# The order of weight loads, a scatter and value loads around batch 1 of an attention and feed-forward kernel

## The chip, the cores and the metric

One core of a Trainium2 chip. The time is device microseconds of one execution of the whole program; of several executions the median is taken. Engines are called as in the profile: PE is TensorE, PEld its weight loads, DVE VectorE, ACT ScalarE, POOL GpSimd, SP SyncE. SP computes nothing here; it issues DMAs. POOL issues DMAs too, and does small copies. ACT issues three at the very start.

## The reference

Attention with a window of 32 to both sides and eight global tokens, followed by a feed-forward layer with a squared ReLU:

```python
batch, n_heads, seq, head_dim = (8, 8, 576, 64)      # 8 global tokens
n_tokens, d_model, d_ff = (4608, 512, 2048)

scores = q @ k.T / sqrt(64)                          # each batch and head
mask = (|pos_q - pos_k| <= 32) | is_global[q] | is_global[k]
attn = softmax(where(mask, scores, -1e9))
x = (attn @ v) -> (4608, 512)                        # heads side by side
out = relu(x @ w_in) ** 2 @ w_out
```

All inputs and the output are float32; the kernel computes in float16 with float32 sums.

## The kernel before

The kernel is one list of calls whose order is written out by hand; each engine runs its own part of that list in order. Attention goes by batch (8), by pair of heads (4 a batch, numbered `i` = 0 to 31 over all batches) and by half of the tokens (2 x 288). The feed-forward layer runs over chunks of 512 or 256 tokens, and its pieces (`mm1`: product with `w_in`, ReLU on ACT, square on DVE; `mm2`: product with `w_out`) stand in a list `fills`, from which the attention loops take some after each step, so that PE always has work. A chunk can start when the batch that it needs is done.

A pair of heads goes so: `sc_mm` (L817) makes scores from `kt` and `qt`, `sc_exp` (L826) the exponentials, `sc_mask` (L836) zeroes what the mask forbids, `pv_mm` (L858) sums values and weights, `pv_rec` (L868, L869) makes reciprocals, `pv_mul` (L902) writes the result to `xT`, the input of the feed-forward layer. `xT` holds it transposed, with one column per token; batch 0's first half first goes to a stand-in, `xA`, of which a part is later copied to `xT` (L1055).

Global tokens attend to everything, so their sums come from all pieces of a batch. `pv_sum` and `pv_globals` collect them (`gs`, `gx`, L877 to L894), and `scatter` (L921 to L924) puts them into the columns of `xT` that belong to the global tokens: eight small copies on POOL, each at a column that is read from a register. Batch 0 is scattered twice into `xA`, by two heads at a time, and once, with all, into `xT` (L1061). The feed-forward products of batch 0's second part (`mm1_half(u, 1)`) read `xT` after that.

The data come in three ways:

- Tokens of batches 0 and 1 (`fetch_tokens`) are loaded in rows and transposed by PE (`transpose`, L534, L540), and DVE and ACT put them into `kt` and `qt` (`place_k`, `place_q`, L549 to L568). The tokens of batch 1 are four loads issued by POOL at L1030 to L1033.
- From batch 2 on, POOL copies k and q of a batch within DRAM, cast to float16 (`fetch_batch`, L191, L198: `kscr`, `qscr`), SP adds the global rows (`fetch_batch_globals`, L206), and SP's DMA transposes bring them into `kt` and `qt` (`fetch_transposed`, L214, L215). The global rows are gathered by POOL (`gather_rows`, L465) and stored in DRAM by SP (`gather_store`, L476) as `gscr`.
- Values of batches 0 and 1 go by `fetch_values` (L165) into `stv`, a staging tile in `early`: for a pair of heads two DMAs of 120 KB (L170) and one of 48 KB (L174), 288 KB in all. DVE casts them from there, pair by pair (`cast_values`, L493, called by `values1`). Rows 0 to 7 of `stv` take the values of the global tokens, broadcast from `gscr` by one DMA (L1064). Values of later batches go by POOL (`fetch_batch_values`, L220, into `stf` or `s16b`).

The weights `w_in` and `w_out` are loaded by POOL in four parts each (L307, L310), and cast on the way. A part of `w_out` is 512 KB in float16. `mm2` of chunk 0 uses the four parts in turn, from part 0 on; sums of its quarters (`weight_sum`, L668) are made on DVE after batch 1.

DMAs that POOL issues use eight completion semaphores in turn, as do those of SP and ACT; one that takes a semaphore again waits until the DMA before it on that semaphore has landed.

A tiny DMA, `gate` (L1063), reads the third part of `w_in`. It has no other use than that SP, which issues in order, waits there until this part has landed; behind it stand the broadcast (L1064) and the values of batch 1 (L1068, L1069). POOL's order there is: two scatters into `xA`, four token loads of batch 1 between them, the four parts of `w_out`, the scatter into `xT`, the gathers for batches 2 and 3 (L1070), a memset, and, from the loop over batch 1, the copies of batch 2.

Of the kernel before, what the change touches and what calls it, by code (L numbers as in the profile page):

```python
# [50 lines left out]
def kernel(  # L51
# [10 lines left out]
    nc = tc.nc  # L62
# [9 lines left out]
    NHP = H // 2  # L72
# [92 lines left out]
    def fetch_values(eng, b, hp, to=None):  # L165
        hs = slice(2 * hp, 2 * hp + 2)
        to = stv[:, :, hs] if to is None else to
        n = NT - 1
        for h in range(2):
            eng.dma_start(  # L170
                out=to[8 : 8 + KT, 0:n, h],
                in_=v[b, 2 * hp + h, 0 : KT * n].rearrange("(t s) d -> s t d", s=KT),
            )
        eng.dma_start(  # L174
            out=to[8 : 8 + KN[n], n],
            in_=v[b, hs, KT * n : S].rearrange("h s d -> s h d"),
        )
# [131 lines left out]
    def fetch_w_out(j):  # L309
        nc.gpsimd.dma_start(out=w_out[:, ts(j, 4), :], in_=wo[:, ts(j, 4), :])  # L310
# [292 lines left out]
    def mm1_half(u, half, tiles=range(NDM)):  # L603

        if 0 not in gts:
            gts[0] = sbt("gt", [P, NFF, TC], FP16)
        if 0 in tiles:
            ph_now[u] = pst("mm", [P, 2, 256])
        ph = ph_now[u]
        for j in range(2):  # L610
            for t in tiles:
                halves(
                    ph[:, j], w_in[:, t, (u + j) * P : (u + j + 1) * P],
                    (xT if half else xA)[:, t, half * 256 : half * 256 + 256],
                    start=(t == 0 and j == 0), stop=(t == NDM - 1), skip_group_check=True,
                )
        if NDM - 1 not in tiles:
            return
        rl = sbt("rl", [P, TC], FP16, bufs=5).rearrange("p (j x) -> p j x", j=2)
        nc.scalar.activation(out=rl, in_=ph, func=AF.Relu)  # L620
        nc.vector.tensor_tensor(
            out=gts[0][:, u : u + 2, half * 256 : half * 256 + 256], in0=rl, in1=rl, op=ALU.mult
        )
# [283 lines left out]
    def pv(i, half):  # L907
        pv_mm(i, half)
        pv_rec(i, half)
        pv_sum(i, half)  # L910
        pv_mul(i, half)
        pv_globals(i, half)
# [8 lines left out]
    def scatter(b, pairs=slice(0, NHP), x=xT):  # L921
        xb = x[:, pairs, b * S : (b + 1) * S]
        for g in range(NG):
            nc.gpsimd.tensor_copy(out=xb[:, :, ds(gv[g], 1)], in_=gxs[b][:, pairs, g : g + 1])  # L924
# [125 lines left out]
        mm1_half(u, 0, range(2))  # L1050
    pv(2, 1)
    pv(3, 1)
    for j in range(2):
        fetch_w_out(j)
    nc.scalar.copy(out=xT[:, :, 256:HS], in_=xA[:, :, 256:HS])  # L1055
    for u in range(0, 8, 2):
        fills.pop(0)
        mm1_half(u, 0, range(2, NDM))
    for j in range(2, 4):
        fetch_w_out(j)  # L1060
    scatter(0)  # L1061
    gate = dram.tile([1, 8], FP16, name="gate")
    nc.sync.dma_start(out=gate, in_=w_in[0:1, 0, 2 * 512 : 2 * 512 + 8])  # L1063
    nc.sync.dma_start(  # L1064
        out=stv[0:NG].rearrange("g t h d -> g t (h d)"),
        in_=gscr[("v", 0)][1].rearrange("g h d -> g (h d)").unsqueeze(1).to_broadcast((NG, NT, dm)),
    )
    for hp in range(NHP):  # L1068
        fetch_values(nc.sync, 1, hp)  # L1069
    gs1 = gather_rows(1)  # L1070
    nc.gpsimd.memset(vbs[0][96:P, NT - 1], 0.0)
# [43 lines left out]
    for i in range(2 * NHP, B * NHP):  # L1115
        b, hp = divmod(i, NHP)
# [65 lines left out]
```

## Time and profile before

| | |
|---|---|
| median of 14 executions | 325.36 us (321.3 to 327.66) |
| the profiled execution | 321.33 us, its span 319.6 us |
| PE, DVE, ACT, POOL busy | 309.4, 245.2, 203.9, 131.3 us |
| `w_out` parts, issue to landing | 14.3 / 16.7 / 19.3 us (least, median, most) |
| POOL waiting in L191 for landings of `w_out` | 7.1 us, three times, at most 2.5 |
| SP waiting in L1064 for the store of the gathered values | 2.3 us |
| POOL waiting in L924 for `gx` of batch 1 | 3.6 us |

A row of a timeline has the start in us from the span's beginning, the duration of the group in us, engine, line, operation, output and inputs, and the count; in brackets the idle time before it and what ended that. An engine with a q (SPq) is its sequencer, which issues DMAs. A DMA's row is its issue, not its transfer. `128*64 128x512` means weights of 128 rows and 64 columns and a result of 128 by 512.

### The profile page before, as it was taken

The numbers are of one execution on the slowest core, as the hardware profiler recorded it, in microseconds if no ns is written. First come the engines' busy times: TensorE is split into PE (matmuls) and PEld (weight loads), VectorE is DVE, ScalarE is ACT, GpSimd is POOL, SyncE is SP. The second block draws the span as 40 slices with busy tenths as digits, with TensorE's granted clock in tenths as the row PEclk, the third lists the DMA queues.
The fourth block names the chain that finished last, engine by engine and source line by source line (L and its number), as shares of the span: only waits on it lengthen the run. The fifth ranks groups of instructions, "written<-read, shape, count | busy, mean of one in ns | idle before, by whom it ended". The sixth has DMA issues, their size and how long they took to land.

```text
span 319.6 us, 11596 instructions
## 1 busy us (share of the span) xinstructions
PE 309.4 (97%) x4821; PEld 235.5 (74%) x4821; DVE 245.2 (77%) x602; ACT 203.9 (64%) x383; POOL 131.3 (41%) x218
## 2 busy tenths in 40 slices
PE   7999999999999999999999999999999999999995
PEld 4677886446699658955998856985698569868995
DVE  6666798598987798778858869876987698668475
ACT  7459777418866786678456487768766876373150
POOL 8918864868911970289200961049302000200000
PEclk9999999999999999999999999999999999999999
DMA  8997999999994999399933699979996301200112
GB/s 192 196 206 130 192 196 153 151 160 154 146 147 119 160 150 115 100 182 111 155 110 77 63 182 124 83 128 173 142 108 123 104 3 35 100 2 2 68 67 68
DMA packets 149493, 38.98 MB, mean 122 GB/s; under 512 B 132697, under 2 KB 148873, under 8 KB 149441
## 3 DMA queue, kind: packets, MB, share of 16 engines
q0 software_dynamic: 97872, 17.08, 70.1%
q1 hardware_dynamic: 51150, 20.57, 34.9%
q8 instruction: 38, 0.62, 0.8%
q10 hardware_dynamic: 418, 0.59, 0.7%
q14 instruction: 15, 0.11, 0.1%
HBM read 37.80 MB, written 17.29 MB: 172 GB/s over the span
## 4 chain that ended last, share of the span: by engine, by line
issue 41%; POOL 20%; PE 19%; DMA 15%; ACT 2%; DVE 1%; POOLq 1%
DMA qscr<-in_q_dram 9%; PE mm L328 7%; DMA w_out<-in_moe_w_out_dram 6%; PE mm_more L328 6%; POOL kscr L191 6%; POOL xT L924 5%; POOL qscr L198 2%; POOL s16b L220 2%; PE at L328 2%; POOL stf L220 1%; PE at L817 1%; PE mm L534 1%; POOLq L924 1%; POOL gstq L465 1%; POOL gstk L465 1%
## 5 line engine op out<-in xcount | busy, mean ns | idle before, releaser
L328 PEld LDWEIGHTS <-w_in 128*64 128x64 f16 (+1 forms) x1288 | 79.3, 109 | 42.7 <-issue 1.2
L328 PE MATMUL mm<-xT,w_in 128*64 128x512 f16 (+2 forms) x608 | 70.9, 352 | 1.0 <-POOL xT L924 1.0
L328 PE MATMUL mm_more<-xT,w_in 128*64 128x512 f16 (+2 forms) x608 | 70.8, 351 | 0.0
L588 DVE TENSOR_TENSOR gt<-rl 128x512 f16<-128x512 f16 x128 | 53.0, 422 | 22.4 <-ACT rl L586 21.3
L328 PEld LDWEIGHTS <-mix 128*64 128x64 f16 x1280 | 68.3, 110 | 2.3 <-DVE mix L674 0.6
L924 POOL COPY xT<-gx 128x4 f16 x64 | 20.2, 315 | 118.2 <-DVE gx L894 114.7
L826 ACT ACTIVATE er<-at 128x880 f16<-128x880 f32 x58 | 49.7, 903 | 20.9 <-PE at L817 20.9
L674 DVE TENSOR_TENSOR mix<-gt 128x1024 f16<-128x1024 f16 (+1 forms) x90 | 54.1, 625 | 0.2
L586 ACT ACTIVATE rl<-mm 128x512 f16<-128x512 f32 x64 | 38.1, 596 | 20.8 <-PE mm L328 20.6
L586 ACT ACTIVATE rl<-mm_more 128x512 f16<-128x512 f32 x64 | 38.3, 599 | 12.5 <-PE mm_more L328 10.7
L836 DVE TENSOR_TENSOR et<-er,mask 128x880 f16<-128x880 f16 x58 | 35.5, 616 | 13.1 <-ACT er L826 12.6
L328 PEld LDWEIGHTS <-gt 128*64 128x64 f16 (+1 forms) x576 | 33.1, 109 | 10.5 <-DVE gt L588 1.4
L868 ACT ACTIVATE rec<-at 128x288 f32<-128x288 f32 x60 | 24.2, 403 | 23.9 <-PE at L858 23.9
L902 DVE TENSOR_TENSOR xT<-at,rec 128x288 f16<-128x288 f32 x59 | 26.8, 454 | 8.8 <-ACT rec L869 8.5
L328 PE MATMUL mm<-early,mix 128*64 128x256 f16 x512 | 31.3, 273 | 0.3 <-DVE mix L674 0.3
L869 ACT ACTIVATE rec<-rec 128x288 f32<-128x288 f32 x64 | 28.4, 443 | 2.0
L191 POOL DMA_DIRECT2D kscr<-in_k_dram x30 | 26.2, 1040 | 7.8 <-DMA w_out<-in_moe_w_out_dram 7.1
L858 PE MATMUL at<-et,onesb 128*64 128x192 f16 (+3 forms) x364 | 27.4, 227 | 0.0
L198 POOL DMA_DIRECT2D qscr<-in_q_dram x24 | 23.8, 1400 | 0.0
L858 PEld LDWEIGHTS <-onesb 128*64 128x64 f16 x400 | 21.9, 110 | 0.7
L817 PEld LDWEIGHTS <-kt 64*128 64x128 f16 x400 | 12.2, 96 | 11.9 <-issue 10.4
L817 PE MATMUL at<-qt,kt 64*128 64x192 f16 (+5 forms) x400 | 19.7, 227 | 0.1
(151 smaller groups left out, 412.6 us busy)
## 6 DMA issues: line engine op xcount, KB each, us to landing
out_dram<-ot SPq DMA_DIRECT2D x32, 256.0 KB
qscr<-in_q_dram POOLq DMA_DIRECT2D x24, 144.0 KB, 7.7
kscr<-in_k_dram POOLq DMA_DIRECT2D x24, 120.0 KB, 6.0
w_in<-in_moe_w_in_dram POOLq DMA_DIRECT2D x4, 512.0 KB, 7.7
w_out<-in_moe_w_out_dram POOLq DMA_DIRECT2D x4, 512.0 KB, 16.7
early<-in_v_dram SPq DMA_DIRECT2D x12, 120.0 KB
stf<-in_v_dram POOLq DMA_DIRECT2D x12, 120.0 KB, 10.1
s16b<-in_v_dram POOLq DMA_DIRECT2D x12, 120.0 KB, 8.3
```

The source lines that it names most:

```text
L191: nc.gpsimd.dma_start(out=kscr[b][r0 : r0 + KN[t]].rearrange("s (h d) -> s h d", d=D), in_=k[b, :, KT * t : KT * t + KN[t]].rearrange("h s ...
L198: nc.gpsimd.dma_start(out=qscr[b][r0 : r0 + GTOK].rearrange("s (h d) -> s h d", d=D), in_=q[b, :, GTOK * g : GTOK * (g + 1)].rearrange("h ...
L328: nc.tensor.matmul(to[r], weights[:, r], moving, **flags)
L586: nc.scalar.activation(out=rl, in_=ph, func=AF.Relu)
L588: nc.vector.tensor_tensor(out=gt[:, :, 0:T], in0=rl, in1=rl, op=ALU.mult)
L674: nc.vector.tensor_tensor(out=gsums[p][:, lo:hi, 0:TH], in0=g[0], in1=g[1], op=op)
L817: nc.tensor.matmul(sc[:, e, so : so + w], kt[r, t, :], qt[r, c0 : c0 + w], start=not added(i, half), stop=True, skip_group_check=True,)
L826: nc.scalar.activation(out=er[:, :, 0:W], in_=scs.pop((i, half))[:, :, 0:W], func=AF.Exp, bias=0.0, scale=scale)
L836: nc.vector.tensor_tensor(out=et[:, :, 0:W], in0=er[:, :, 0:W], in1=mask[:, MB[half] : MB[half] + W].unsqueeze(1).to_broadcast((P, 2, W)), ...
L858: nc.tensor.matmul(acc[D * e : D * e + D, x, o : o + w], onesb if x else vt[:, t, e], et[:, e, so : so + w], start=(n == 0), stop=(n == le ...
L869: nc.scalar.activation(out=rec, in_=rec, func=AF.Exp, scale=-1.0)
L924: nc.gpsimd.tensor_copy(out=xb[:, :, ds(gv[g], 1)], in_=gxs[b][:, pairs, g : g + 1])
```

## The change

The four `w_out` parts are issued in one loop behind the last scatter of batch 0, where two and two stood ahead of it. On POOL nothing else stood between these four issues: the copy at L1055 is ACT's and the products between are PE's, so POOL's new order is scatter, four loads, gathers. Of the values of batch 1, the three DMAs of the first pair of heads are issued by SP right behind `gate`, ahead of the broadcast of the global rows; the other nine stay behind it. No instruction is added or removed, and the number of DMAs of each queue and the completion semaphores of those behind the broadcast stay as they were.

```diff
     pv(2, 1)
     pv(3, 1)
-    for j in range(2):
-        fetch_w_out(j)
     nc.scalar.copy(out=xT[:, :, 256:HS], in_=xA[:, :, 256:HS])
     for u in range(0, 8, 2):
         fills.pop(0)
         mm1_half(u, 0, range(2, NDM))
-    for j in range(2, 4):
+    scatter(0)
+    for j in range(4):
         fetch_w_out(j)
-    scatter(0)
     gate = dram.tile([1, 8], FP16, name="gate")
     nc.sync.dma_start(out=gate, in_=w_in[0:1, 0, 2 * 512 : 2 * 512 + 8])
+    fetch_values(nc.sync, 1, 0)
     nc.sync.dma_start(
         out=stv[0:NG].rearrange("g t h d -> g t (h d)"),
         in_=gscr[("v", 0)][1].rearrange("g h d -> g (h d)").unsqueeze(1).to_broadcast((NG, NT, dm)),
     )
-    for hp in range(NHP):
+    for hp in range(1, NHP):
         fetch_values(nc.sync, 1, hp)
```

## The prediction

> **What bounds the kernel now.** I read the page's busy shares first, then the list of what TensorE (PE) waited for, then the order of instructions on GpSimd (POOL) and SyncE (SP) around the edited lines, then PE at the places that use what these two deliver. From the page:
>
> ```profile
> span 319.6 us, 11596 instructions
> PE 309.4 (97%) x4821; PEld 235.5 (74%) x4821; DVE 245.2 (77%) x602; ACT 203.9 (64%) x383; POOL 131.3 (41%) x218
> ```
>
> PE is busy for all but 10.2 us. What an edit between 23 and 70 us can win in this execution is what PE waits there. The list of PE's waits, from 20 to 75 us (total, times, longest), begins:
>
> ```profile
> PE mm L328 <- DVE qt L568: 0.7, 1, 0.7
> PE mm L328 <- POOL xT L924: 0.6, 1, 0.6
> ```
>
> The first is a PSUM eviction on DVE at 55 us. The second is batch 1's scatter, at 71 us. Neither names a DMA, SP, the scatter of batch 0 or `w_out`; the rest of that list adds 1.1 us, all on DVE and ACT. So the ceiling of a gain in the profiled execution is 0.7 + 0.6 + 1.1 = 2.4 us, and none of it hangs directly on what is moved. POOL, in order of time (start, us, line, what, count, idle before and its releaser):
>
> ```profile
> 28.84 2.74 POOL L924 COPY mix<-gx 128x2 f16 x8
> 31.71 3.00 POOL L310 DMA_DIRECT2D w_out<-in_moe_w_out_dram  x4
> 34.67 2.62 POOL L924 COPY xT<-gx 128x4 f16 x8
> 37.64 1.03 POOL L465 DMA_INDIRECT gstk<-in_k_dram,gidx  x1 [0.36 <-issue]
> ...
> 47.01 0.87 POOL L191 DMA_DIRECT2D kscr<-in_k_dram  x1 [2.30 <-DMA w_out<-in_moe_w_out_dram]
> 50.22 0.87 POOL L191 DMA_DIRECT2D kscr<-in_k_dram  x1 [2.34 <-DMA w_out<-in_moe_w_out_dram]
> 53.54 0.76 POOL L191 DMA_DIRECT2D kscr<-in_k_dram  x1 [2.45 <-DMA w_out<-in_moe_w_out_dram]
> ```
>
> The `w_out` issues and the scatter stand back to back and change places. The three waits show that POOL later idles 7.1 us for landings of `w_out`: a copy of batch 2 takes the completion semaphore of a `w_out` load, eight DMAs back. SP:
>
> ```profile
> 23.27 0.24 SPq L1063 DMA_DIRECT2D gate<-w_in  x1
> 25.96 0.28 SPq L1064 DMA_DIRECT2D early<-gscr_v  x1
> 26.29 0.86 SPq L170 DMA_DIRECT2D early<-in_v_dram  x2
> ...
> 40.12 1.31 SPq L174 DMA_DIRECT2D early<-in_v_dram  x1
> ```
>
> SP stands idle from 23.51 to 25.96, until the stored global rows have landed. The DMA engines' busy share from 22 to 28 us (40 slices of 0.15 us) is low in the same stretch:
>
> ```profile
> DMA  9999999999999997372211110000000081258599
> ```
>
> From about 24.4 to 26.8 us they do little; from 27.8 to 66 us they are full. And PE at the consumers:
>
> ```profile
> 38.33 0.37 PE L817 MATMUL at<-qt,kt 64*128 64x160 f16 x6
> 38.62 1.05 PE L328 MATMUL mm<-xT,w_in 128*128 128x256 f16 x8
> ...
> 50.80 1.04 PE L328 MATMUL mm<-w_out,gt 128*128 128x512 f16 x4
> ...
> 70.69 0.56 PE L817 MATMUL at<-qt,kt 64*128 64x160 f16 x12
> 71.88 1.05 PE L328 MATMUL mm<-xT,w_in 128*64 128x512 f16 x8 [0.63 <-POOL xT L924]
> ```
>
> **The scatter ahead of the weights.** It needs the last two products into `xT` (L902, the second 32.64 + 0.46 = 33.10) and ACT's copy (L1055, over at 32.80). So POOL, free at 31.58, idles 1.6 us, starts at about 33.2 and with the same 2.62 us ends at 35.9, where it ended at 37.29: 1.4 earlier. Its reader is the product at 38.62, which follows 0.3 us of L817 that waited for a DVE eviction, and shows no wait for the scatter. Gain: nothing, hidden by the eviction of pair 4; without that cover it would be at most 1.4.
>
> **The weights behind it.** Four issues, 3.00 us, run from 35.9 to 38.9 instead of 31.71 to 34.70: 4.2 later. Next on POOL come three gathers (from 39.3 instead of 37.64, 1.6 later), the memset, and two copies of batch 2, which end near 46.3 instead of 44.7. The next three copies waited to 47.01, 50.22, 53.54 anyway, so these 1.6 us fall into POOL's own 7.1. What counts is when `w_out` lands. Issue to landing is 14.3, 16.7 and 19.3 us for the last three: 46.7, 49.9, 53.3, each 3.3 after the other, which is a queue being worked off, not the latency of one. Ahead of them on that queue are the tokens of batch 1; by the completion counts in the trace the last of these lands between 35.9 (first engine) and 39.1 (last). If the first `w_out` is issued by 36.7, the queue hardly runs dry, and the landings stay. Bounds: 0 late (backlog covers all), or the whole 4.2. PE reads the first quarter of `w_out` at 50.80; by the spacing it lands near 43.4, so even 4.2 more leaves 3 us. The second quarter is read at 57.8, the third at 63.7. Directly, nothing. Indirectly, copies, transposes and the scores of batch 2 (L817 at 70.69) hang on the last landing; the completion counts of that first `qt` transpose end at 69.45, 1.2 us ahead of PE. So the price is between 0 and 4.2 - 1.2 = 3.0 us; I take 0, as the tokens' landing row is the nearest.
>
> [...]
>
> **The first values of batch 1.** Three DMAs (120 + 120 + 48 KB) move past one broadcast. SP issues them at 23.5 to 24.9 (0.86 + 0.47 us) in the idle stretch; their space is free, since batch 0's cast of these heads is long over. Broadcast: still 25.96. The nine other value loads start 1.4 us earlier (26.3 instead of 27.7). The engines get 0.29 MB of work into the hole; at the 200 GB/s of the full slices that is 1.4 us, by which everything behind it in the full stretch can come earlier. First reader is the DVE cast at 39.76, which waits for no DMA; the last values land at 54.2 by their counts, their cast is at 56.64. So in the profile the gain is 0; it deepens a slack. Bounds: 0, and -1.4 if in other executions PE does wait behind this stretch. I take -0.3, nearer the profile.
>
> **DVE and POOL side by side.** The scatter now runs beside the first squares (L621, five of 0.42 us from 33.33), the weight issues beside the eviction of pair 4 (36.36 to 38.27), on which PE waits at 38.33. Scatter copies took 0.20 to 0.42 us at 34.67, but up to 1.21 beside the 1.2 us sums of L668 at 66 us. Upper bound: five squares held 0.2 us each, 1.0 us on PE; lower 0, as the old order had the same neighbours for half the time. I take 0.2.
>
> [...]
>
> **Sum.** 0 + 0 - 0.3 + 0.2 = -0.1 us. The profiled execution took 321.33 us; by the profile alone the changed kernel takes 321.2. The median of 14 runs is 325.36, 4.0 above it, and ten of the 14 lie between 324.89 and 327.66. What these 4 us are, one profile cannot tell. A candidate ahead of the change is PE's start:
>
> ```profile
> 12.66 0.64 PE L328 MATMUL at<-idle 128*64 128x512 f16 x1
> ...
> 17.33 0.38 PE L328 MATMUL at_more<-idle 128*64 128x512 f16 x2
> ```
>
> The same 512 columns take 0.64 us at 12.7 and 0.38 at 17.3, though the page's clock row says full speed all along. If this step comes later in other executions, they are some us longer whatever stands behind 23 us. I forecast 325.0: the median less that tenth, rounded down towards the larger of the two one-sided cases.
>
> **Rivals.** *Faster.* The 4.0 us between median and profile are PE waiting behind the full DMA stretch, whose slacks are only 1.2 us (transposes) and 2.4 us (last values) in the profile. The last values gain most: with a quarter of SP's stream gone from a stretch in which that stream gets a fifth of the bytes, they land some 6 us earlier. The gain is 1.4 (324.0) to 4.0 (321.4); middle 322.7. Against it: no wait of PE for a DMA in the profile, and the late step of PE's speed as another cause. *Slower.* POOL's queue runs dry at 36 to 39 us, the late issue is carried through to the third copy of batch 2 and its transposes, and PE stands at L817 near 70.7. It decides once the last `w_out` lands after 53.3 + 1.2 = 54.5; price up to 3.0: 328.4. Against it: SP's stream fills the engines meanwhile, and 1.4 us of work went into the hole. *No effect through contention.* DVE and POOL delay each other by the full bound: +1.0, 326.4, still inside half a per cent.
>
> **How the numbers follow.** A difference below 0.5%, 1.6 us, can't be told from no change here. No change: 0.45, with 324.0 to 326.9. Faster: 0.30. Slower: 0.25, of which 0.17 the dry queue and 0.08 contention beyond its bound, or a new wait I don't see. The range runs from 321.8, which the larger part of the faster case reaches, to 328.0, most of the dry queue's price.
>
> **What would show it.** Right: the scatter at 33.2, the `w_out` issues at 36 to 39, POOL's three waits still ending on `w_out`, at 46 to 53.5 or earlier; value loads on SP from 23.5; no DMA among PE's waits. Wrong: a wait before L817 at 70 us, the third `w_out` wait ending after 54.5, or a median near 322 with the same PE waits as now.

## The result and the profile after

| | before | after |
|---|---|---|
| median | 325.31 us (47 executions, 320.7 to 327.66) | 319.86 us (10, 318.94 to 321.1) |
| ratio | | 0.9885, 95% interval 0.9847 to 0.9923 |
| profiled execution, its span | 321.33, 319.6 | 319.95, 318.2 |

The changed kernel is faster by about 1.2% in the ratio and by 5.4 us in the median, below the forecast range, and its executions lie closer together. The ratios leave out executions more than 1.5% above a kernel's shortest, so where these are common the medians differ by more than the ratio says.

The page of the changed kernel, first lines (11598 instructions, where before has 11596: two semaphore instructions of SP come with the moved value loads):

```profile
span 318.2 us, 11598 instructions
PE 307.3 (97%) x4821; PEld 234.2 (74%) x4821; DVE 245.0 (77%) x602; ACT 204.0 (64%) x383; POOL 131.3 (41%) x218
```

POOL after, in order of time (columns as before):

```profile
31.89 3.27 POOL L924 COPY xT<-gx 128x4 f16 x8 [1.90 <-DVE xT L902]
35.09 3.00 POOL L310 DMA_DIRECT2D w_out<-in_moe_w_out_dram  x4
...
46.11 0.87 POOL L191 DMA_DIRECT2D kscr<-in_k_dram  x1 [1.68 <-DMA w_out<-in_moe_w_out_dram]
49.07 0.87 POOL L191 DMA_DIRECT2D kscr<-in_k_dram  x1 [2.09 <-DMA w_out<-in_moe_w_out_dram]
52.07 0.76 POOL L191 DMA_DIRECT2D kscr<-in_k_dram  x1 [2.13 <-DMA w_out<-in_moe_w_out_dram]
```

The scatter waits for the last product into `xT`, the weights stand behind it, and the three waits for their landings end 0.9 to 1.5 us earlier than before. SP after:

```profile
23.92 0.96 SPq L170 DMA_DIRECT2D early<-in_v_dram  x2
24.97 1.25 SPq L174 DMA_DIRECT2D early<-in_v_dram  x1
26.98 0.27 SPq L1063 DMA_DIRECT2D early<-gscr_v  x1
```

The first pair's values use the stretch in which SP stood. PE, at the start and where batch 2 begins:

```profile
12.85 0.40 PE L328 MATMUL at<-idle 128*64 128x512 f16 x1
...
70.48 1.05 PE L328 MATMUL mm<-xT,w_in 128*64 128x512 f16 x8 [0.63 <-POOL xT L924]
```

In this execution PE is at full speed by 12.85 us (0.40 us for 512 columns), where before's profiled execution still took 0.64 at 12.66. That is where these two profiles differ. PE's wait for ACT's `et` ended at 27.27 us before and at 25.93 after, the wait in the last line above at 71.88 and 70.48. Between the two lie 44.61 us before and 44.55 after (this stretch serves as a measure again below). The stretch with the whole change in it is no shorter, and PE waits in it for the same things as long as before. So the two profiles alone do not show where the 5.4 us of the median come from.

### The profile page after: what moved, and what is told of

Read it like the earlier page. It is cut to its first block, busy times and chain, and to the rows that moved or that the text cites. A ratio compares the mean times of both kernels' runs of the same rounds, so it can differ in the third digit from the quotient of the medians.

```text
span 318.2 us, 11598 instructions
## 1 busy us (share of the span) xinstructions
PE 307.3 (97%) x4821; PEld 234.2 (74%) x4821; DVE 245.0 (77%) x602; ACT 204.0 (64%) x383; POOL 131.3 (41%) x218
## 4 chain that ended last, share of the span: by engine, by line
issue 40%; PE 21%; POOL 17%; DMA 16%; ACT 2%; DVE 1%; POOLq 1%
DMA qscr<-in_q_dram 10%; PE mm L328 9%; PE mm_more L328 7%; POOL xT L924 6%; POOL kscr L191 5%; DMA w_out<-in_moe_w_out_dram 5%; POOL s16b L220 2%; POOL stf L220 2%; DMA stf<-in_q_dram 2%; PE at L328 1%; POOL qscr L198 1%; POOLq L924 1%; PE at L817 1%; PE mm L534 1%; POOL w_out L310 1%
## 5 line engine op out<-in xcount | busy, mean ns | idle before, releaser
L586 ACT ACTIVATE rl<-mm 128x512 f16<-128x512 f32 x64 | 38.1, 596 | 20.8 <-PE mm L328 20.6
L902 DVE TENSOR_TENSOR xT<-at,rec 128x288 f16<-128x288 f32 x59 | 26.8, 454 | 9.0 <-ACT rec L869 8.5
L817 PEld LDWEIGHTS <-kt 64*128 64x128 f16 x400 | 12.0, 95 | 11.5 <-issue 10.5
L817 PE MATMUL at<-qt,kt 64*128 64x192 f16 (+5 forms) x400 | 19.5, 225 | 0.1
```

The source lines that it names most:

```text
L817: nc.tensor.matmul(sc[:, e, so : so + w], kt[r, t, :], qt[r, c0 : c0 + w], start=not added(i, half), stop=True, skip_group_check=True,)
```

## The experiments

The kernels of each paragraph below ran on one chip, beside executions of the kernel before; the first three paragraphs share a chip, the fourth and the fifth have one each (second and third chip). Theories: A, PE waits behind the full DMA stretch of 27 to 70 us in the longer executions of before; B, only the late step of PE's speed makes them long; C, PE waits there for the scatter. D came out of the first runs: an early start of PE makes POOL issue the token loads of batch 1 ahead of the values, and DVE, then PE, stand until the values land.

**The kernel before, a longer execution.** Unchanged.

> The unchanged kernel once more, for a profile of one of its longer executions (33 of 47 took 324.0 us or more). Theory A (PE waits behind the full DMA stretch of 27 to 70 us in these executions): the profile shows some 4 us of PE waits between 35 and 72 us that the first profile did not have, on a DMA, on DVE casts of the values or before L817 at about 70 us. Theory B (the step of PE's speed at the start comes later): no new wait behind 24 us; the 512-column product at about 17 us still takes 0.6 us instead of 0.38, and all of PE's work is shifted by some 4 us from 24 us on. Median 325.3 by both.

Median 327.83 us, beside 325.43 for the same kernel (ratio 1.0052, 0.9999 to 1.0106); the profiled execution took 327.8. (Of the 47 executions, 35 took 324.0 us or more.) First POOL and DVE in the first profile, then POOL, SP and DVE in this one:

```profile
26.12 0.66 POOL L160 DMA_DIRECT2D s16b<-in_k_dram  x1 [0.19 <-issue]
```

```profile
39.76 0.82 DVE L493 CAST early<-early 128x512 f16<-128x512 f32 x2
...
44.76 0.56 DVE L493 CAST early<-early 128x512 f16<-128x512 f32 x2
```

```profile
23.08 0.66 POOL L160 DMA_DIRECT2D s16b<-in_k_dram  x1 [0.20 <-issue]
...
29.59 3.00 POOL L310 DMA_DIRECT2D w_out<-in_moe_w_out_dram  x4
```

```profile
26.32 1.79 SPq L170 DMA_DIRECT2D early<-in_v_dram  x2
```

```profile
39.72 0.78 DVE L493 CAST early<-early 128x512 f16<-128x512 f32 x1 [1.78 <-DMA early<-in_v_dram]
40.99 0.23 DVE L493 CAST early<-early 104x128 f16<-104x128 f32 x1 [0.50 <-DMA early<-in_v_dram]
...
47.69 0.43 DVE L493 CAST early<-early 128x512 f16<-128x512 f32 x1 [2.20 <-DMA early<-in_v_dram]
49.16 0.23 DVE L493 CAST early<-early 104x128 f16<-104x128 f32 x1 [1.04 <-DMA early<-in_v_dram]
```

and PE:

```profile
51.43 0.26 PE L858 MATMUL at<-et,early 128*64 128x160 f16 x2 [3.17 <-DVE xT L902]
```

The casts that waited for nothing in the first profile wait 5.5 us here, and PE 3.17 us behind DVE. What released PE is `xT` (L902), which stands behind the late casts in DVE's order and ended at 51.37 us; the waits of those casts name the DMA. So A holds here, by way of the casts. B falls in this execution: the trace's clock record puts the step of PE's speed at 5.3 us here, at 16.3 us in the first profile, so the longer execution is the one that starts early. The tokens are issued at 23.08 us, 3.2 us ahead of the values; in the first profile it was 26.12, level with them. `w_out` too is issued earlier, at 29.59 instead of 31.71 us.

**Each part alone, and the changed kernel once more.**

```diff
# values alone
+    fetch_values(nc.sync, 1, 0)
     nc.sync.dma_start(
...
-    for hp in range(NHP):
+    for hp in range(1, NHP):
```

> Only the values of the first pair go ahead of the broadcast; the weights stay ahead of the scatter. Theory A: most of the gain, 320 to 322 us, since the value stream lands some 6 us earlier. Theory B: nothing behind 23 us matters; 325.3, or the same as the changed kernel only by chance of the start. Theory C (it is the scatter that PE waits for in the longer executions): 325.3.

```diff
# scatter alone
-    for j in range(2):
-        fetch_w_out(j)
...
-    for j in range(2, 4):
+    scatter(0)
+    for j in range(4):
         fetch_w_out(j)
-    scatter(0)
```

> Only the scatter goes ahead of the four weight loads; the values stay behind the broadcast. Theory A: little, 324 to 326 us. Theory B: 325.3. Theory C (in the longer executions the weight issues on POOL are held up and PE waits at 38 us for the scatter behind them): the whole gain, 319.9 us.

> The changed kernel beside the others on one chip: 319.9 us by all theories, if it is the change; Theory B would let its executions spread as those of before do (320.7 to 327.7).

Beside 325.43 us for before: values alone 322.50 (0.9913, 0.988 to 0.9947), scatter alone 324.03 (0.9976, 0.9935 to 1.0017), the changed kernel 323.97 (0.9969, 0.9922 to 1.0015). On this chip the gain of the whole change is not clear of nothing, and the 319.9 us expected of the changed kernel were not reached. In none of the three profiles does DVE wait for a DMA between 36 and 62 us, in the last two with the step of PE's speed at 7.3 and 7.0 us. C falls: no profile has PE waiting for the scatter of batch 0.

**Two pairs ahead, values held back, values alone again.**

```diff
# two pairs (with weights first, and with the scatter first)
+    for hp in range(2):
+        fetch_values(nc.sync, 1, hp)
     nc.sync.dma_start(
...
-    for hp in range(NHP):
+    for hp in range(2, NHP):
```

> Values of two pairs (six DMAs) ahead of the broadcast, weights ahead of the scatter as before. Theory D (in the longer executions of before the token loads of batch 1 are in the DMA engines ahead of the values, DVE stands in its casts of the values and PE behind it): the values are ahead of the tokens in every execution, no wait of DVE for values, 0.985 to 0.995 of before, all executions within 2 us; equal to the run with one pair moved or up to 1 us shorter. Theory A' (it is the amount of work moved into the idle stretch of the engines that counts): another 1 us shorter than with one pair.

> As the run with two pairs, and the scatter ahead of the weights. Theory D: the values are early already, so the scatter's place adds nothing (within 1 us of the run with two pairs). Theory C' (the scatter's place has a gain of its own): 1 to 3 us below it.

```diff
# values behind tokens: before, with SP held
+    held = dram.tile([1, 8], FP16, name="held")
+    nc.sync.dma_start(out=held, in_=token_rows("k", NHP)[0:1, 0, 0:8])
     for hp in range(NHP):
         fetch_values(nc.sync, 1, hp)
```

> The kernel before, with SP held by one more tiny DMA, behind the broadcast, until the first token load of batch 1 has landed (27 to 30 us): all values of batch 1 go behind the token loads in every execution. Theory D: every execution is one of the longer ones, 1.005 to 1.015 of before's median, DVE waits for values by 5 us or more in its profile, PE by 3 us or more near 50 us. Theory B (only the start decides): as before, 1.000, with its spread.

> Only the first pair moved, once more beside the others: 0.991 of before (0.988 to 0.995 on the chip before).

Beside 326.49 us for before: two pairs 324.32 (0.9942, 0.9909 to 0.9974), two pairs with the scatter first 325.14 (0.9936, 0.9891 to 0.998), values held back 328.21 (1.0055, 1.0004 to 1.0105), values alone 322.66 (0.9889, 0.9811 to 0.9967). DVE with the values held back:

```profile
41.25 0.43 DVE L493 CAST early<-early 128x512 f16<-128x512 f32 x1 [3.15 <-DMA early<-in_v_dram]
```

It waits there for values by 7.4 us in all; the shortest of ten executions took 326.03, where before has some at 324. That is D's test from the other side. Two pairs were expected to be as good as one and are not. DVE in that run:

```profile
40.69 0.56 DVE L493 CAST early<-early 128x512 f16<-128x512 f32 x2 [3.60 <-DMA early<-gscr_v]
```

The values are there, but the broadcast of the global rows, which the same cast reads, now stands behind six loads, and the cast waits for it. The six loads that were moved up pushed another transfer back: the broadcast is issued at 27.78 us here, at 25.96 in the first profile. That this is what two pairs lose against one is not shown: only 0.30 us of a wait of PE follow DVE's 3.60, and the same profile has 3.4 us at half the clock from 40.0 us on. With two pairs ahead the scatter's place adds nothing (325.14 and 324.32), so C' falls.

**All parts on another chip.**

> The changed kernel, the value part alone and the scatter part alone side by side on one chip. Theory D (each part alone keeps the values from being late; DVE waits for nothing else there): all three within 0.5% of each other, 0.985 to 0.995 of before. Theory E (the scatter's place has a price where the weight issues then stand beside PE's densest stretch at 35 to 42 us): the changed kernel 1 to 1.5 us behind the value part alone, as on the chip of the earlier runs (323.97 and 322.50).

> Theory D: as the changed kernel within 0.5%. Theory E: 1 to 1.5 us faster than it; 0.989 to 0.991 of before by both.

> Theory D: no wait of DVE for values, 0.990 to 0.998 of before. Theory E: the slowest of the three, 0.995 to 1.000 of before.

```diff
# values first: values alone, and ahead of the gate
+    fetch_values(nc.sync, 1, 0)
     gate = dram.tile([1, 8], FP16, name="gate")
     nc.sync.dma_start(out=gate, in_=w_in[0:1, 0, 2 * 512 : 2 * 512 + 8])
-    fetch_values(nc.sync, 1, 0)
```

> The first pair's values go ahead of the gate too, so some 2 us earlier than in the value part alone, beside the last parts of w_in; the weights ahead of the scatter as before. Theory D: nothing waits for values any more, so no further gain: within 0.3% of the value part alone. A gain of 1 us or more would show that the values' place is not the whole of it.

Beside 325.10 us for before: the changed kernel 319.92 (0.989, 0.9826 to 0.9955), values alone 319.59 (0.986, 0.98 to 0.9921), scatter alone 320.29 (0.9881, 0.9818 to 0.9945), values first 319.74 (0.9878, 0.9814 to 0.9941). Either part alone has the whole gain; together they have it once. Theory E (the scatter's place has a price) finds nothing here; on the first chip values alone was 1.5 us ahead of the changed kernel. There PE waits between 38 and 43 us for nothing that the profile names, 0.4 to 1.3 us in all, in all eight profiles (0.97 in the kernel before, 0.45 and 0.47 in values alone, 0.83 in scatter alone, 1.10 in the changed kernel); no profile made elsewhere shows it there. So it is not the scatter's place alone that brings it; what does stays open. Values still earlier add nothing.

**What makes the values late.**

> One more profile of the kernel before. Theory D: if the step of PE's speed comes before 12 us, the token loads are issued at 23 to 24 us, DVE waits for values by 3 us or more and the time is 325 or more; if it comes at 16 us, the tokens are issued at 26 us, no such wait, 321 to 322. Theory F (the delay of the values has nothing to do with the start): waits and start are not tied.

> The same once more: the wait of DVE for values goes with an early step and with token loads issued ahead of the values (D), or does not (F).

```diff
# no warm products (idle products, not part of the output)
-    keep_warm(4)
+    keep_warm(0)
     index_base()
     gb = indices()
-    keep_warm(4)
+    keep_warm(0)
```

> The kernel before without the two groups of four idle warm-up products at the start (L937, L940); they have no part in the output. PE's speed steps up later, at 16 us or more. Theory D: the token loads then always come at 26 us or later, level with the values; DVE never waits for values, and although PE starts slower the median is below that of before, 0.987 to 0.995. Theory B (a late step is what makes executions long): 1.003 to 1.01 of before.

```diff
# tokens late
     for nm in "kq":
         fetch_tokens(pool, nm, NHP)
-    for nm in "kq":
-        fetch_tokens(pool, nm, NHP + 1, NHP - 1)
...
     scatter(0, slice(2, NHP), xA)
+    for nm in "kq":
+        fetch_tokens(pool, nm, NHP + 1, NHP - 1)
```

> The kernel before, with the two large token loads of batch 1 (432 KB each) behind the second scatter into xA instead of ahead of it, so 2.7 us or more later. Theory D: no wait of DVE for values, 0.987 to 0.993 of before, unless PE then waits for these tokens at 38 us (then 0.993 to 1.000). Theory F: 1.000.

The two more profiles of before took 321.57 and 321.42 us, with the step at 16.0 and 15.8 us, the tokens at 26.09 and 25.99 and no wait of DVE for a DMA. With the first profile and the long one that makes four of four in which start, token issue and wait go together; only one of the four is of the early kind. Of the 17 other executions of before on this chip no profile was made, but each has its mean granted clock: the six with 0.999 or 1.000 took 320.87 to 324.54 us, the eleven with 0.995 or less 324.77 or more.

The two edits do more. With the tokens late, the median is 320.01 beside 325.11 (0.9899, 0.9836 to 0.9962): POOL in this run, whose PE is at full speed from 8.6 us on,

```profile
23.32 0.66 POOL L160 DMA_DIRECT2D s16b<-in_k_dram  x1 [0.19 <-issue]
...
27.13 2.66 POOL L924 COPY mix<-gx 128x2 f16 x8 [2.51 <-DVE mix L902]
29.83 0.74 POOL L160 DMA_DIRECT2D s16b<-in_k_dram  x1
...
31.28 3.00 POOL L310 DMA_DIRECT2D w_out<-in_moe_w_out_dram  x4
```

issues the first two token loads as early as the long execution, the two large ones behind the values, and DVE waits for no DMA. Nothing was done to the values. The weights' place in the order is the old one too, but they are issued 1.7 us later than in the long execution (31.28 instead of 29.59), since the moved token loads now stand ahead of them; so this run alone does not part tokens from weights.

Without the warm-up products, nine of twelve executions took 320.94 to 322.31 us and three 325.63 to 326.17, median 322.15 (the ratio, 0.9974, 0.9926 to 1.0023, is unclear); of the 17 of before, four took less than 322 us. Work of PE at the start was taken away, its first 5.5 us left nearly empty, and most executions became shorter, not longer: B's order of things is turned round. D's forecast was missed as well, since it said that DVE would never wait. The profile is of one of the three long ones. In it the step comes at 11.7 us, not at 16 or later, the tokens are issued at 24.37, DVE waits 4.2 us for values, and PE

```profile
49.95 0.34 PE L858 MATMUL at<-et,early 128*64 128x160 f16 x2 [3.44 <-DVE xT L902]
```

around and after which the stretches of that execution (PE, PEld, DVE, ACT, POOL busy with counts, granted clock, DMA share, GB/s) read:

```profile
46.00:50.00 4.00, 0.56 (x10) 0.32 (x10) 2.75 (x9) 0.28 (x1) 0.99 (x2) 0.91 1.27 183
50.00:56.00 6.00, 6.00 (x37) 3.66 (x37) 4.50 (x13) 4.21 (x8) 4.08 (x5) 0.50 1.81 154
56.00:60.00 4.00, 3.60 (x84) 2.27 (x82) 2.46 (x6) 1.87 (x5) 3.23 (x5) 0.99 2.37 156
```

In this execution two costs stand together: 3.44 us of idle PE, and, from 2.7 us into that wait on, 6.8 us at a clock of 0.50, worth about 3.4 us of work. PE's stretch from the wait for `et` to that for batch 1's scatter is 51.09 us here and 44.62 in the run with late tokens: a difference of 6.5, about the sum of the two.

Side by side, with the times at which the traces' completion counts have the values of the first and of the second pair landed (all in us):

| profile | step | large token loads | `w_out` | values landed | DVE waits for values | PE's stretch |
|---|---|---|---|---|---|---|
| before, the first one | 16.3 | 27.39 | 31.71 | 31.7, 38.7 | 0 | 44.61 |
| before, longer (first chip) | 5.3 | 24.35 | 29.59 | 40.9, 49.1 | 5.5 | 49.90 |
| without warm-ups (third chip) | 11.7 | 25.64 | 29.82 | 39.2, 47.6 | 4.2 | 51.09 |
| values alone (first chip) | 7.2 | 24.68 | 29.77 | 31.9, 40.9 | 0 | 45.49 |
| values alone (second chip) | 5.1 | 24.33 | 29.58 | 32.4, 40.2 | 0 | 44.60 |
| scatter alone (first chip) | 7.3 | 24.67 | 34.55 | 37.0, 43.2 | 0 | 47.89 |
| changed kernel (second chip) | 7.0 | 24.68 | 34.63 | 32.4, 37.3 | 0 | 44.56 |
| tokens late (third chip) | 8.6 | 29.83 | 31.28 | 30.6, 32.6 | 0 | 44.62 |

Where tokens and weights are both early and the values have their old place, the values of the first pair land 7.5 to 9.2 us later than in the first profile, and DVE waits. Moving the values alone ends that, moving the weights alone does, and moving the tokens does, which takes the weights along. Scatter alone issues its tokens 0.3 us behind the long execution's and the values no earlier (from 27.00 us); only `w_out` comes 5 us later, and DVE does not wait. So D is too narrow where it names the tokens alone: early tokens without early weights did no harm. Whether early weights alone would, no run shows. On the first chip scatter alone still has a stretch 3.3 us over the first profile's, with half the clock for 3.4 us from 41.5 us on and 0.83 us of the unnamed waits in it.

## Why the prediction was wrong

**The step that failed** is in the part on the first values: "First reader is the DVE cast at 39.76, which waits for no DMA", and from it "I take -0.3, nearer the profile". The sentence is true of the execution that was profiled, and of two others, but not of the one profiled later in which the start came early. There the casts wait 5.5 us. I had the bounds 0 and -1.4 from the work that fits into the idle stretch. The right size is what PE stands for the values, 3.2 to 3.4 us, plus half of the time at the lower clock where it falls, up to 3.4 us more; on the first chip, where it did not fall, the stretch is 49.90 us in the long execution and 45.49 with the values moved, 4.4 us apart. Of the forecast's cases it is the rival *Faster* that happened, by the mechanism it named, values late behind the full stretch, and to beyond its far end of 321.4. One thing the rival had otherwise: it is the first two pairs that are late, not the last values. A second step failed with it: the scatter's and the weights' places were put at nothing, and scatter alone measured 0.9881 on the second chip (0.9976, unclear, on the first).

**The median's 4.0 us.** I put them down, loosely, to a late step of PE's speed. The sign was wrong. An early step makes an execution shorter where no values are late: with the step at 7.0 and 11.2 us the changed kernel has spans of 318.1 and 318.2 (on the first chip, where this kernel takes longer, 322.9 with the step at 7.0); with it at 16.5 scatter alone has 319.9, and no profile of the changed kernel has so late a step. PE's wait for `et` ends 1.3 us or more sooner with an early step. But in the kernel before it lets the token loads go ahead of the values, with the weights close behind, and costs 4.4 us or more. So the three short executions of before that were profiled all had a slow start, and one of them was the profile I worked from. The change makes the fast start pay: by these profiles, 325.31 to 319.86 is the lost wait and clock, and the early start kept.

**What held.** For an execution like the profiled one the sum, -0.1 us, was right: 44.61 and 44.55 us between the two waits above. The scatter does wait for L902 and delays nobody; it began 1.90 us, not 1.6, after POOL came free, and took 3.27 us instead of 2.62. `w_out` was issued from 35.09 to 38.1 us, and its landings did not follow the issue: by the completion counts they came at 42.2 to 51.8 us, where they had come at 42.5 to 53.3, so that issuing them 3.4 us later (35.09 us instead of 31.71) cost nothing here. Contention of DVE and POOL: PE's wait at the first scores of pair 4 is 0.14 us in both profiles. The dry queue, the *Slower* rival, did not show: no profile has PE waiting before L817 at 70 us.

**What I did not see.** The scatter's part was costed by who waits for the scatter, and the weights by who waits for the weights. What it does is a third thing: 4 MB of weight reads come to the engines 3 to 5.5 us later (35.09 us against 31.71 and 29.59), and in that time the values go through: in scatter alone the second pair's had landed at 43.2 us instead of 49.1. That is why scatter alone can have the gain as well, and why moving the weights later is no loss here. On the second chip, where scatter alone was faster, its profile is of a late start (16.5 us), so there the gain was timed and not traced. My own list of what would prove me wrong had the case in it, "a median near 322 with the same PE waits as now"; the median came to 319.86, with those waits.

**Open.** Why on the first chip the changed kernel gains only 0.3% (unclear) while values alone gain 0.9 to 1.1% on it; the unnamed PE waits at 38 to 43 us, and waits of PE for ACT of 0.5 to 1 us between 81 and 87 us, which all profiles of that chip have and no others, lie beside it, but no run was made on them. Whether every long execution of before is one with an early start was seen in one profile and by three edits, not in each execution. Nor was it tested what each of the large token loads and of the weight loads adds, or a weight load moved by itself. The ranking of values alone ahead of the changed kernel is not settled: their ratios on the second chip, 0.986 and 0.989, have intervals that overlap.

## What to carry to other kernels

When the executions of a kernel spread by more than a change is worth, one profile is one of several orders of events; profile a long one too before a wait is called absent, and look at which DMAs are issued first in each. With the DMA engines full, as in the first profile from 27.8 us on, the place of a transfer was a question of what it goes ahead of: bulk loads that nobody needs for 13 us or more, issued 2 to 3 us earlier, made urgent ones land some 9 us later here. A test that moves the competitor (late tokens, late weights) is as telling as one that moves the victim, but look at what else it moves.

## What the runs showed of the hardware

The speed of PE stepped up at 5.1 to 16.6 us after the start in the profiles made here, for the same instructions up to there in most of these kernels; the page's clock row shows full speed all along, since the record begins with the step. The matmul durations, 0.64 and 0.40 us for 512 columns, show it.

By the clock records of all these traces the granted clock changes at whole multiples of 3.41 us after the step (1, 2, 9 to 11, 79 to 94 of them): after the step it held for 303.79 us, 89 of them, in the first profile, and for 307.20 us, 90, in the profile of the changed kernel. A wait of PE of 3.44 us (46.51 to 49.95, in the run without the warm-up products) saw the clock fall to 0.50 at 49.2 us, 2.7 us into it, for 6.8 us; one of 3.17 us in the long execution of before (48.26 to 51.43) did not. Counted in these steps, the first covers 2.7 us of one interval, the second 1.4 and 1.7 us of two. That a wait brings the fall, and that its place counts and not only its length, is my reading of these two executions and was not shown. PE still worked for 0.7 us of the interval ahead of the fall, and four profiles of the first chip, with mean granted clocks of 0.994 and 0.995, have 3.4 us of half clock between 40 and 47 us behind waits of 0.2 to 2.0 us, which no run here explains. The step at the start, with gaps between the products, came 3.8 to 15.4 us after PE's first product at 1.26 us (8.0 us after the one at 3.71 without the warm-up products).
